# Grouped-query attention on one core: the second tile's K load issued from ScalarE's queue

## Chip, cores and metric

One core of one Trainium2 chip. The metric is device time in microseconds (us) of one launch; lower is better. Before the change the median of 3 runs is 337.94 us (337.85 to 338.18).

## The reference

Attention with 32 query heads that share 8 K/V heads. Only 16 queries per head stand against 2048 keys, so nearly all bytes are K and V (134 MB in bf16).

```python
B, Hq, Hkv, Sq, Sk, D = 16, 32, 8, 16, 2048, 128
k = jnp.repeat(k, Hq // Hkv, axis=1)
v = jnp.repeat(v, Hq // Hkv, axis=1)
scores = jnp.einsum("bhqd,bhkd->bhqk", q, k) * D ** -0.5
p = softmax(scores, axis=-1)
return jnp.einsum("bhqk,bhkd->bhqd", p, v)
```

## The kernel before

The 128 pairs of batch and K/V head are taken two at a time: 64 tiles. A tile needs 1 MB of K and 1 MB of V, and 64 query rows for each of its two heads. The program is written out per engine; semaphores alone order the engines against each other.

For each tile, VectorE transposes K in 32-blocks from `Kd` to `KT` (`kt`, line 421), TensorE forms the scores into `S_ps` (`scores`, line 277), VectorE scales and negates them into `Sneg` and takes the minimum (line 431), ScalarE forms the exponentials into `P` (line 495), TensorE transposes these into `ST_ps` (`turn_p`, line 288), ScalarE copies them to `PT` (line 504), and TensorE multiplies them with V into `O_ps` (`pv`, line 301). ScalarE then divides by the row sums (line 527). Two tiles form a pair: their V loads share one of the two buffers of `Vd`, which come free when the products of the pair before last are formed (`sem_pv`).

Q comes in 16 chunks of 128 KB for four tiles each. GpSimd copies a chunk four times over into `Q4` (line 180), having waited for the load (`sem_q`) and for TensorE's transposes of the chunk before (`sem_qt[1]`); TensorE transposes half a chunk at a time (`turn_q`, line 264) and ScalarE copies the result to `QT` (`q_out`, line 480).

Loads and stores are DMAs, each put into the ring of the engine that issues it. SyncE issues nearly all of them, in the order of a loop over time steps t: K of tile t (`load_k`, line 191; `Kd` has eight slots, so the first eight need no wait, and each later one waits until the transpose of the tile eight before it is done, `sem_kt`), then a chunk of Q (`load_q`, line 217), stores, and V of an earlier tile (`load_v`, line 209; V of tile p goes at t = p + 2 for the first two, p + 6 for the next two, then up to 11 behind). SyncE's first issues are thus K0, K1, K2, Q2, V0, K3, V1, K4 and so on. V of tile 4 is the first V load that has to wait for a buffer. The last six tiles' V go into slots of `Kd`.

ScalarE issues two DMAs only: chunks 0 and 1 of Q, at its very start (line 534), before its table load and its first copies `q_out`. Each load has a semaphore of its own slot that rises by 16 when all has landed (`sem_k[1]` for the K slot of tile 1). VectorE's program begins with `kt(0)` and `kt(1)`, which wait for `sem_k[0]` and `sem_k[1]`, and goes on with the minimum of tile 0, the transpose of tile 2, the minimum of tile 1, and so forth.

Of the kernel before, what the change touches and what calls it, by code (L numbers as in the profile page):

```python
# [6 lines left out]
ALU = mybir.AluOpType  # L7
# [22 lines left out]
def bass_standalone__gqa_softmax__sampling_kernel(  # L30
# [16 lines left out]
    NU = B * Hkv // 2  # L47
# [15 lines left out]
    Kd = sb("Kd", [128, NK, 32 * D], BF16)  # L63
# [21 lines left out]
    sem_k, sem_kt = ring("sem_k", NK), ring("sem_kt", NK)  # L85
# [14 lines left out]
    kf = k.rearrange("b h s d -> (b h s d)").rearrange("(n g i a x) -> n i a g x", n=ND, g=2, i=2, a=64)  # L100
# [4 lines left out]
    def v_lag(p):  # L105
        return 2 if p < 2 else 6 if p < 4 else max(VLAG, 11 - max(p - 6, 0) // 8)
# [11 lines left out]
    for d in range(WHOLE):  # L118
        t = 2 * d + SLAG + v_lag(2 * d + 4)
# [17 lines left out]
    def v_tile(u):  # L137
        return Kd[:, u - T0, :].rearrange("p (g x) -> p g x", g=2)
# [29 lines left out]
    with nc.Block() as block:  # L168
# [16 lines left out]
        @block.sync  # L185
        def _(sp):
            def load_k(m):
                s = m % NK
                if m >= NK:
                    sp.wait_ge(sem_kt[s], m // NK)  # L190
                sp.add_instruction(mybir.InstDMACopy(  # L191
                    name=nc.get_next_instruction_name(), engine=mybir.EngineType.SP,
                    ins=sp.lower_ap_dma(kf[m // 2, m % 2]), outs=sp.lower_ap_dma(Kd[:, s, :].unsqueeze(1)),
                    queue="qSPDynamicHW", mode="Copy", cce_op=ALU.bypass,
                )).then_inc(sem_k[s], 16)

            def load_v(p):
                d, g = divmod(p, 2)
                if p >= T0:
                    sp.wait_ge(sem_kt[p - T0], ROUNDS)  # L200
                    if p < NU - 1:
                        sp.dma_start(v_tile(p), vt[d, g]).then_inc(sem_vt[p - T0], 16)  # L202
                        return
                    for x, (y, lo, hi) in enumerate(LAST_V):
                        sp.dma_start(v_tile(p)[:, y, D * lo:D * hi], vt[d, g, :, y, D * lo:D * hi]).then_inc(sem_vl[x], 16)
                    return
                if d >= NV and g == 0:
                    sp.wait_ge(sem_pv[d % NV], d // NV)
                sp.dma_start(Vd[d % NV][:, g, :, :].rearrange("a j d -> a (j d)"), vf[p]).then_inc(sem_v[d % NV], 16)

            def load_q(c):
                s = c % NQ
                if c >= NQ:
                    sp.wait_ge(sem_q4, c - NQ + 1)
                rows = 128 * QPAIRS
                src = qf[rows * c:rows * (c + 1), :].rearrange("(a j) d -> a j d", j=QPAIRS)
                sp.dma_start(Qn[s][:, :, :], src).then_inc(sem_q[s], 16)

            def store(d, i, g):
                if i == g == 0:  # L220
                    sp.wait_ge(sem_nm[d % NV], normed(d))
                rows = slice(64 * g, 64 * (g + 1))
                sp.dma_start(of[d, i, g], o_sb(d)[rows, i, :]).then_inc(sem_o[d % NO], 16)  # L223

            for t in range(LASTT):
                if t < NU:
                    load_k(t)
                for c in range(2, NQC):
                    if t == max(c, QPAIRS * c - QLEAD):
                        load_q(c)  # L230
                for d, i in store_at.get(t, []):
                    store(d, i, 0)
                for p in v_behind[t]:
                    load_v(p)
                for d, i in store_at.get(t, []):
                    store(d, i, 1)
            for d in range(WHOLE, ND - 1):
                if d < T0 // 2:
                    sp.wait_ge(sem_nm[d % NV], normed(d))
                else:  # L240
                    sp.wait_ge(sem_end, 2 * d + 2 - T0)
                for g in range(2):
                    dst = of[d, :, g].rearrange("i x d -> x i d")
                    sp.dma_start(dst, o_sb(d)[64 * g:64 * (g + 1), :, :]).then_inc(sem_out, 16)
            for i in range(2):
                for g in range(2):
                    sp.wait_ge(sem_end, TILES - 1 + i * (g + 1))
                    sp.dma_start(of[ND - 1, i, g], o_sb(ND - 1)[64 * g:64 * (g + 1), i, :]).then_inc(sem_out, 16)
            for s in range(NO):
                sp.wait_ge(sem_o[s], 64 * ((WHOLE - s + NO - 1) // NO))  # L250
            sp.wait_ge(sem_out, 32 * (ND - WHOLE + 1))
# [224 lines left out]
        @block.scalar  # L476
        def _(act):
            def q_out(x, n):
                act.wait_ge(sem_qt[x], n)
                act.activation(  # L480
                    QT[x][:, :, :].rearrange("p b (a j) -> p b a j", j=QPAIRS),
                    q_ap().rearrange("p b (j a) -> p b a j", j=QPAIRS), ACT.Copy,
                ).then_inc(sem_qe[x], 1)

            def exp(i, alone):
                n = J // 2
                pb, sneg = P[i // 2 % NP][:, :].bitcast(BF16), Sneg[i % 2][:, :]
                for h in range(2 if alone else 1):
                    if alone:
                        dst = pb[:, J * 64 * (i % 2):J * 64 * (i % 2 + 1)].rearrange("p (t y h e) -> p h t y e", t=n // 2, h=2, e=2)[:, h]  # L490
                        src = sneg.rearrange("p (h t e y) -> p h t y e", h=2, t=n // 2, e=2)[:, h]
                    else:
                        dst = pb.rearrange("p (n i y e) -> p i n y e", n=n, i=2, e=2)[:, i % 2]
                        src = sneg.rearrange("p (n e y) -> p n y e", n=n, e=2)
                    ins = act.activation(  # L495
                        dst, src, ACT.Exp, bias=nbias[:, i:i + 1], scale=-1.0,
                        accum_out=rowsum[:, ROUND * h + i:ROUND * h + i + 1],
                    )
                ins.then_inc(sem_exp[i % STEP], 1)

            def p_out(i, n):
                for h in range(2):
                    act.wait_ge(sem_pt[h][i % STEP], n)
                    ins = act.activation(  # L504
                        PT[i % NPT][:, 4 * h:4 * (h + 1), :].rearrange("p t q -> p (t q)"),
                        ST_ps[:, 512 * h:512 * (h + 1)], ACT.Copy,
                    )
                ins.then_inc(sem_po[i % STEP], 1)

            def emit(at):  # L510
                for i in range(ROUND):
                    act.wait_ge(sem_max[i % STEP], at.tile(i))
                    exp(i, at.end and i >= T0 % ROUND)
                    if i % 2 == 0 and not (at.end and i >= 4):
                        y = (i + 4) // 2
                        q_out(y % 2, at.num(2, y // 2 + 1))
                    if at.first or i >= TLAG:
                        p_out(i - TLAG, at.tile(i - TLAG))
                    if i % 2 and (at.first or i >= PVLAG + 1) and not (at.end and i == ROUND - 1):
                        y = (i - PVLAG - 1) // 2  # L520
                        act.wait_ge(sem_pv[y % NV], at.num(2, y // NV + 1))
                        extra = at.end and WHOLE <= ROUND // 2 * (ROUNDS - 1) + y
                        if not extra and (at.first >= 2 or (at.first == 1 and y >= 0)):
                            act.wait_ge(sem_o[y % NO], at.num(64, 64 * (y // NO)))
                        for z in range(2):
                            x = (2 * y + z) % ROUND
                            ins = act.activation(Osb[y % NO + (NO if extra else 0)][:, z, :], o_ap(z), ACT.Copy,  # L527
                                                 scale=rrec[:, x:x + 1])
                        ins.then_inc(sem_nm[y % NV], 1)

            for c in range(2):
                rows = 128 * QPAIRS
                src = qf[rows * c:rows * (c + 1), :].rearrange("(a j) d -> a j d", j=QPAIRS)
                act.dma_start(Qn[c][:, :, :], src).then_inc(sem_q[c], 16)
            for x in range(2):
                q_out(x, 1)
            in_rounds(act, 2, ROUNDS - 1, emit)
            for u in range(NU - TLAG, NU):
                p_out(u, TURNS)
# [28 lines left out]
```

## Time and profile before

| | us or share |
|---|---|
| median of 3 runs | 337.94 |
| profiled execution | 337.78 |
| its span in the profile | 335.9 |
| PE busy (matmul) | 282.2 (84%) |
| VectorE busy | 292.1 (87%) |
| ScalarE busy | 261.8 (78%) |
| GpSimd busy | 31.3 (9%) |
| SyncE's DMA ring (q1): packets, MB | 31632, 138.17 |
| ScalarE's DMA ring (q10): packets, MB | 288, 0.26 |
| DMA over the span | 412 GB/s |
| K load, issue to landing (median) | 11.3 |
| V load, issue to landing (median) | 9.7 |

The span runs from the first to the last instruction that the hardware profiler recorded; the rest of the time lies around it. Busy times are sums over the span, and engines overlap. PE is TensorE's matmul side, PEld its weight load; DVE is VectorE, ACT ScalarE, POOL GpSimd, SP SyncE. Rows with a q behind the engine (SPq, ACTq) are its issues of DMAs, not the movement of the data; the time to landing is from the issue until the data's semaphore is complete, and so contains the wait behind earlier loads of the ring. A DMA share can come out a little over 1 where records overlap. In a row of the timeline the brackets give how long the engine had been idle and what ended that.

### The profile page before, as it was taken

What the parts mean: (1) busy time and instruction counts of PE and PEld (TensorE: products, weight loads), DVE (VectorE), ACT (ScalarE), POOL (GpSimd) and SP (SyncE); (2) the same over time, 40 slices, a digit from 0 to 9 for tenths busy, and PEclk for the clock granted to TensorE, in tenths of its full rate; (3) what the DMA queues carried; (4) which work ended last, traced back from release to release, by engine and by line L of the source; (5) the groups of instructions that cost most, each with busy time, mean ns of one, the idle gap of its engine ahead of it and who ended that gap; (6) DMA issues with size and microseconds to landing.
All of it is one profiled execution on the core that took longest, in us unless ns stands there. A gap on an engine that the chain in (4) does not pass through costs nothing.

```text
span 335.9 us, 14877 instructions
## 1 busy us (share of the span) xinstructions
PE 282.2 (84%) x6720; PEld 164.5 (49%) x6720; DVE 292.1 (87%) x232; ACT 261.8 (78%) x357; POOL 31.3 (9%) x22
## 2 busy tenths in 40 slices
PE   1755888889888889889888898898888889887995
PEld 1323445544554555455445554554455455454484
DVE  2999899998889999999999999999989889889641
ACT  2365888888777889888888888888888877888871
POOL 3202020200202020020202001020201002000000
PEclk9959899999999999999999999999999999999999
DMA  7999999999999999999999999999999999999996
GB/s 300 423 418 417 418 420 416 420 424 424 417 425 423 419 422 422 425 419 413 425 422 421 419 421 424 424 417 420 423 421 424 421 423 424 422 424 424 411 415 212
DMA packets 31930, 138.55 MB, mean 412 GB/s; under 512 B 12464, under 2 KB 14768, under 8 KB 16304
## 3 DMA queue, kind: packets, MB, share of 16 engines
q1 hardware_dynamic: 31632, 138.17, 100.0%
q10 hardware_dynamic: 288, 0.26, 0.2%
q8 instruction: 5, 0.08, 0.1%
q14 instruction: 5, 0.04, 0.0%
HBM read 136.31 MB, written 2.10 MB: 412 GB/s over the span
## 4 chain that ended last, share of the span: by engine, by line
DMA 36%; PE 32%; ACT 15%; SPq 8%; DVE 5%; issue 4%
DMA Vd<-in_v_dram 29%; PE S_ps L277 13%; PE ST_ps L288 9%; PE O_ps L301 9%; ACT P L495 8%; DMA Kd<-in_v_dram 5%; SPq L223 4%; ACT PT L504 3%; DVE Sneg L431 3%; DMA Kd<-in_k_dram 2%; DVE KT L421 2%; ACT QT L480 2%; ACT O L527 2%; SPq L191 2%; SPq L202 1%
## 5 line engine op out<-in xcount | busy, mean ns | idle before, releaser
L495 ACT ACTIVATE P<-Sneg,nbias 128x2048 bf16<-128x2048 f32 (+1 forms) x70 | 161.9, 2315 | 4.1 <-DVE Sneg L431 4.1
L431 DVE TENSOR_SCALAR_CACHE_REDUCE Sneg<-S_ps 128x2048 f32<-128x2048 f32 x64 | 145.3, 2270 | 18.4 <-PE S_ps L277 18.4
L421 DVE STREAM_TRANSPOSE KT<-Kd 128x2048 f32<-128x2048 f32 x64 | 147.4, 2303 | 13.9 <-DMA Kd<-in_k_dram 13.9
L277 PE MATMUL S_ps<-KT,QT 32*64 32x512 bf16 x2048 | 127.7, 623 | 22.3 <-DVE Sneg L431 19.8
L504 ACT ACTIVATE PT<-ST_ps 128x512 f32<-128x512 f32 x128 | 69.6, 595 | 52.2 <-PE ST_ps L288 51.8
L288 PE MATMUL ST_ps<-ident,P 128*128 128x128 f32 x512 | 69.6, 279 | 14.3 <-ACT QT L480 9.6
L301 PEld LDWEIGHTS O_ps<-Vd,PT 64*64 64x64 bf16 x3712 | 54.2, 107 | 37.2 <-issue 36.2
L301 PE MATMUL O_ps<-Vd,PT 64*64 64x128 bf16 x3712 | 63.2, 218 | 8.3 <-DMA Vd<-in_v_dram 8.3
L288 PEld LDWEIGHTS ST_ps<-ident,P 128*128 128x128 f32 x512 | 54.8, 141 | 23.4 <-issue 20.5
L277 PEld LDWEIGHTS S_ps<-KT,QT 32*64 32x64 bf16 x2048 | 29.3, 115 | 73.7 <-issue 45.7
L180 POOL COPY Q<-Qn 128x2048 bf16<-128x2048 bf16 x16 | 30.3, 1896 | 248.9 <-PE ST_ps L264 247.6
L264 PEld LDWEIGHTS ST_ps<-ident,Q 64*128 64x128 f32 x256 | 20.0, 150 | 32.3 <-issue 32.3
L264 PE MATMUL ST_ps<-ident,Q 64*128 64x64 f32 x256 | 24.6, 242 | 5.1 <-POOL Q L180 5.1
L480 ACT ACTIVATE QT<-ST_ps 128x512 f32<-128x512 f32 x32 | 19.5, 610 | 9.3 <-PE ST_ps L264 9.2
L527 ACT ACTIVATE O<-O_ps,rrec 128x128 bf16<-128x128 f32 x56 | 17.7, 376 | 0.0
L495 ACT ACTIVATION_READ_ACCUMULATOR P<-Sneg,nbias 128x1 f32 x70 | 14.4, 206 | 0.0
L431 DVE DVE_READ_ACCUMULATOR Sneg<-S_ps 128x1 f32 x64 | 5.4, 84 | 0.0
L449 DVE TENSOR_SCALAR O<-O_ps,rrec 128x128 bf16<-128x128 f32 (+1 forms) x5 | 1.7, 348 | 3.5 <-PE O_ps L319 2.9
L449 DVE TENSOR_SCALAR O<-S_ps,rrec 128x128 bf16<-128x128 f32 x4 | 1.3, 349 | 3.9 <-PE S_ps L319 3.9
L439 DVE RECIPROCAL rrec<-rowsum 128x2 f32<-128x2 f32 x29 | 4.6, 160 | 0.0
L319 PE MATMUL S_ps<-Kd,PT 128*64 128x128 bf16 x128 | 4.1, 220 | 0.0
L319 PEld LDWEIGHTS S_ps<-Kd,PT 128*64 128x64 bf16 x128 | 3.7, 110 | 0.5 <-issue 0.5
(11 smaller groups left out, 8.2 us busy)
## 6 DMA issues: line engine op xcount, KB each, us to landing
Kd<-in_k_dram SPq DMA_DIRECT2D x64, 1024.0 KB, 11.3
Vd<-in_v_dram SPq DMA_DIRECT2D x58, 1024.0 KB, 9.7
Kd<-in_v_dram SPq DMA_DIRECT2D x5, 1024.0 KB, 13.4
Qn<-in_q_dram SPq DMA_DIRECT2D x14, 128.0 KB, 10.6
out_dram<-O SPq DMA_DIRECT2D x112, 16.0 KB, 9.7
Kd<-in_v_dram SPq DMA_DIRECT2D x1, 512.0 KB, 16.7
Qn<-in_q_dram ACTq DMA_DIRECT2D x2, 128.0 KB, 3.8
Kd<-in_v_dram SPq DMA_DIRECT2D x1, 256.0 KB, 14.1
```

Source lines behind the costliest of these rows:

```text
L180: gp.tensor_copy(Q4[:, :, :, :, :].rearrange("p j b r x -> p (j b) r x"), src.unsqueeze(2).to_broadcast([128, 2 * QPAIRS, 4, 64]),).then_i ...
L223: sp.dma_start(of[d, i, g], o_sb(d)[rows, i, :]).then_inc(sem_o[d % NO], 16)
L264: ins = pe.transpose(q_ap()[:, b, 64 * j:64 * (j + 1)], src[rows, j, b, :], ident[rows, rows])
L277: ins = pe.matmul(S_ps[64 * g:64 * (g + 1), 512 * r:512 * (r + 1)], qt[rows, b, e, at:at + 64], kt[rows, b, e, g], start=(acc == 0), stop= ...
L288: ins = pe.transpose(ST_ps[:, 512 * h + 128 * t:512 * h + 128 * (t + 1)], P[w // 2 % NP][:, 128 * y:128 * (y + 1)], ident[:, :])
L301: ins = pe.matmul(o_ap(i)[64 * g:64 * (g + 1), :], pt[rows, j % 16 // 2, j % 2, 64 * g:64 * (g + 1)], Vd[d % NV][rows, g, j, :], start=(j ...
L421: dve.transpose(KT[u % 2][:, :].rearrange("p (b j a) -> p j b a", b=2, j=J), Kd[:, u % NK, :].bitcast(F32).rearrange("p (j b c) -> p j b c ...
L431: dve.tensor_scalar(Sneg[i % 2][:, :].rearrange("p (j r a) -> p r j a", j=J, r=4), S_ps[:, :].rearrange("p (r j a) -> p r j a", j=J, r=4), ...
L480: act.activation(QT[x][:, :, :].rearrange("p b (a j) -> p b a j", j=QPAIRS), q_ap().rearrange("p b (j a) -> p b a j", j=QPAIRS), ACT.Copy, ...
L495: ins = act.activation(dst, src, ACT.Exp, bias=nbias[:, i:i + 1], scale=-1.0, accum_out=rowsum[:, ROUND * h + i:ROUND * h + i + 1],)
L504: ins = act.activation(PT[i % NPT][:, 4 * h:4 * (h + 1), :].rearrange("p t q -> p (t q)"), ST_ps[:, 512 * h:512 * (h + 1)], ACT.Copy,)
L527: ins = act.activation(Osb[y % NO + (NO if extra else 0)][:, z, :], o_ap(z), ACT.Copy, scale=rrec[:, x:x + 1])
```

## The change

SyncE's loop skips K of tile 1. ScalarE issues that load, with the same source, destination, size and semaphore, into its own ring between its loads of Q chunks 0 and 1. Everything else stays.

```diff
             for t in range(LASTT):
-                if t < NU:
+                if t < NU and t != 1:
                     load_k(t)
...
                 act.dma_start(Qn[c][:, :, :], src).then_inc(sem_q[c], 16)
+                if c == 0:
+                    act.add_instruction(mybir.InstDMACopy(
+                        name=nc.get_next_instruction_name(), engine=mybir.EngineType.Activation,
+                        ins=act.lower_ap_dma(kf[0, 1]), outs=act.lower_ap_dma(Kd[:, 1, :].unsqueeze(1)),
+                        queue="qActDynamicHW", mode="Copy", cce_op=ALU.bypass,
+                    )).then_inc(sem_k[1], 16)
```

## The prediction

> **What bounds the kernel now.** First the page's slices, then stretches of the start beside one of the middle. The first two lines below are the 40 slices (tenths of the 16 DMA engines; GB/s); the others are stretches (length, busy of PE, PEld, DVE, ACT, POOL, granted clock, DMA share, GB/s).
>
> ```profile
> DMA  7999999999999999999999999999999999999996
> GB/s 300 423 418 417 418 420 416 420 424 424 417 425 423 419 422 422 425 419 413 425 422 421 419 421 424 424 417 420 423 421 424 421 423 424 422 424 424 411 415 212
> ...
> 2.00:3.00 1.00, 0.00 (x0) 0.00 (x0) 0.00 (x0) 0.91 (x1) 0.00 (x0) 1.00 1.17 327
> 3.00:4.00 1.00, 0.00 (x0) 0.00 (x0) 0.00 (x0) 0.00 (x0) 0.94 (x1) 1.00 0.82 296
> 4.00:5.00 1.00, 0.00 (x0) 0.00 (x0) 0.00 (x0) 0.00 (x0) 0.96 (x1) 1.00 1.02 420
> 160.00:240.00 80.00, 72.89 (x1819) 42.00 (x1823) 75.16 (x58) 68.18 (x94) 8.09 (x5) 1.00 1.02 422
> ```
>
> The reader is to see one resource that never rests: from the second slice to the last but one the DMA engines are nine tenths busy or more, at some 421 GB/s. A K or V load of 1.05 MB takes 2.49 us at that rate, a tile (one of each) 4.98 us, while VectorE, the busiest compute engine, works 2.31 + 2.27 + 0.08 = 4.66 us a tile. So the end is set by the stream: when it starts, its bytes, whether it ever runs dry, and the tail behind the last V. The change moves none of the bytes and nothing at the tail.
>
> Second, the timeline of the start: issues, then the two K transposes that wait for the loads, then the transpose of tile 4.
>
> ```profile
> 0.72 0.87 ACTq L534 DMA_DIRECT2D Qn<-in_q_dram  x2
> 0.73 1.97 SPq L191 DMA_DIRECT2D Kd<-in_k_dram  x3
> 6.23 2.31 DVE L421 STREAM_TRANSPOSE KT<-Kd 128x2048 f32<-128x2048 f32 x1 [6.23 <-DMA Kd<-in_k_dram]
> 8.98 2.31 DVE L421 STREAM_TRANSPOSE KT<-Kd 128x2048 f32<-128x2048 f32 x1 [0.44 <-DMA Kd<-in_k_dram]
> 11.88 1.90 POOL L180 COPY Q<-Qn 128x2048 bf16<-128x2048 bf16 x1 [6.92 <-PE ST_ps L264]
> 22.94 2.31 DVE L421 STREAM_TRANSPOSE KT<-Kd 128x2048 f32<-128x2048 f32 x1 [0.39 <-DMA Kd<-in_k_dram]
> ```
>
> K0 releases VectorE at 6.23, K1 at 8.98; from there VectorE has no gap until tile 4, whose K it waits 0.39 us for.
>
> Third, SyncE's timeline where loads first wait for computation (V of tiles 4, 6 and 8, each held until the products of an earlier pair of tiles free a buffer of Vd).
>
> ```profile
> 50.71 0.33 SPq L209 DMA_DIRECT2D Vd<-in_v_dram  x1
> ...
> 60.31 0.33 SPq L209 DMA_DIRECT2D Vd<-in_v_dram  x1
> ...
> 69.88 0.33 SPq L209 DMA_DIRECT2D Vd<-in_v_dram  x1
> ```
>
> The list of DMA issues, taken over each of these moments alone, gives issue to landing: 8.3, 8.7 and 9.5 us. K0, issued into empty queues, took 5.5 us. The difference is work still queued ahead when the gate opens: 2.8, 3.2 and 4.0 us. That is how late computation may become before the stream runs dry.
>
> **The change part by part.**
>
> *SyncE loses one issue.* Three K issues take 1.97 us, so one is 0.66, and K2, Q2, V0 and what follows are issued 0.66 us earlier. This is worth nothing: they stand in SyncE's ring behind 1.05 MB of K0, and by 9.73 us SyncE is held by a full ring (the issue of a V there takes 2.13 us instead of 0.48).
>
> *ScalarE gains one issue.* Its two Q issues end at 0.72 + 0.87 = 1.59; with 0.66 more at 2.25. Behind it stands the table load (1.28 us, from 1.62), then to 3.56 at the latest. ScalarE's next work begins at 6.22, when it has waited 3.32 us for TensorE: 2.66 us of cover. Cost 0; without cover 0.66.
>
> *K1 shares the engines with K0 instead of following it.* The trace has no K load in ScalarE's ring, so the price comes from Q1, which stands where K1 will. The DMA queues over 4.2 to 5.4 us (packets, MB, share):
>
> ```profile
> q1 hardware_dynamic: 52, 0.42, 82.5%
> q10 hardware_dynamic: 53, 0.05, 12.7%
> ```
>
> q1 is SyncE's ring with K0 (8 KB packets), q10 ScalarE's with Q1 (1 KB): one packet of each in turn. Q1's first packets come at 3.9 us; before, from 2.6 to 3.9, q10 moved none. By 3.9 us 59 of K0's 128 packets had gone (16 in 1.5 to 2.6, 43 after). If K1 begins at 3.9 too, K0's other 69 packets alternate with 69 of K1: 69 x 8192 B / 421 GB/s = 1.34 us more, less some 0.19 us for Q1's packets that no longer lie between. K0 lands 1.15 us later: the first transpose starts at 7.38 and ends at 9.69. K1's last 59 packets then alternate with K2's: 59 x 8192 / 421 GB/s = 1.15 us more, less Q1's whole 0.35: K1 lands 0.8 us later, its transpose starts at 9.78. VectorE's unbroken row thus begins 0.8 us late.
>
> The bounds: if K1 begins together with K0, K0 comes up to 2.49 - 0.19 = 2.3 us later, the transposes start at 8.53 and 10.84: 1.86 late. If it begins only when K0 is done, it alternates with all of K2: 2.49 - 0.35 = 2.1 late. If its packets keep their old order, 0, and K0 gains the 0.19. So -0.2 to +2.1, and I take 0.8, by the row that is nearest.
>
> The Trainium skill (DMA: Bandwidth & Descriptors, Queues, rings and completion order) says that an engine drains a whole packet of typically 9 to 17 descriptors from one ring before it turns to the other; by that K1's eight pieces on an engine would go in one block, and K0 would be up to 2.5 us late, an estimate that leaves the sum where it is. The one-to-one row above doesn't agree with it.
>
> *Q1 stands behind K1.* It landed at 6.35 (issue 1.15 + 5.2). Now its 8 packets on each engine follow K1 and alternate with K2's and V0's: 8 x 0.35 us (2.49 / 8 for the large one, 0.04 for its own) behind 9.75, so about 12.5. GpSimd reads it at 11.88 + 0.8 = 12.7 at the earliest, since it waits for TensorE; its copy takes 1.90 and TensorE uses the result at 15.60 + 0.8. Cost 0; Q1 would have to land after 14.5 to cost anything.
>
> *Where the lateness goes.* 0.8 us late at tile 1; 0.39 of it falls into the wait at tile 4, as K4's landing hardly moves (the bytes ahead of it are the same). The first gate opens about 0.4 to 0.8 us late, against 2.8 us of queued work: the stream doesn't run dry, V4 and all later loads move at their old times. Behind it the lateness shrinks: gates lie 9.60 and 9.57 us apart, while four loads with their Q and outputs take the stream 9.96 or more, so 0.4 us a pair is made up; the trace shows TensorE waiting for V itself three times between 60 and 100 us (2.5 us in all). K loads that wait for transposes have more cover: the one issued at 39.97 landed 16.6 us later.
>
> *Sum.* Stream start 0, bytes 0, gaps 0, tail 0: against the profiled execution 335.9 us of span plus 1.88 around it = 337.78, which is 0.16 under the median of the runs, 337.94. I forecast no change, 337.9 us. One per cent is 3.4 us; what a measurement here can tell from no change is about 0.2%, 0.68 us.
>
> **Rivals.**
>
> *The stream runs dry at the first gate (slower).* It decides from a delay of 2.8 + 0.39 = 3.2 us at tile 1, and each further us costs one. For: the chain of waits runs through computation from K1's landing to 70 us, PE's granted clock is 0.58 in 15 to 20 and 0.76 in 20 to 40 us, and TensorE once idles 2.10 us there with nothing shown that it waits for; a shifted start could meet such a stall twice. Against: the bound of the landings is 2.1. Price: 2.1 + 2.1 - 3.2 = 1.0 us, 338.9. Were nothing absorbed at all, 0.8 to 2.1 us: 338.7 to 340.0.
>
> *The start fills better (faster).* From 2 to 4 us the engines moved 327 and 296 GB/s against 421: 219 kB missing, 0.52 us. If two rings of large packets fill that, the whole stream moves forward: 337.4. For: the DMA share of 0.82 in 3 to 4 us, when q10 was empty. Against: the share is 1.17 the stretch before, with both rings at work and still 327 GB/s, so the slowness is in the packets. Beyond 0.2% it needs a part of the first 2 us too. The Trainium skill (same page, Issuing engines are not separate DMA queues) speaks against any gain: issuing from two engines saves only the sequencer's time.
>
> *The landings don't move.* K1's descriptors come so late that its packets keep their order: also 337.9, without the delay at the first transposes.
>
> **How the numbers follow.** Forecast 0.59; unmoved landings 0.08; better start 0.14, of which half stays within 0.2%; stream dry 0.19, nearly all of it beyond 0.2%. A little of the forecast's own share is scatter to either side. Faster 0.09, same 0.70, slower 0.21. The range runs from 337.2, a little beyond the full start gain, to 338.9, the dry stream's price.
>
> **What would show it.** Right: first transposes at about 7.4 and 9.8; V4 issued within 1 us of 50.71, its landing sooner behind its issue by the same amount; no slice under nine tenths; last V landing at the old time. Wrong: a dip in GB/s at 50 to 56 us (dry stream), over 327 and 296 GB/s at 2 to 4 us (better start), transposes still at 6.23 and 8.98 (nothing moved), or a Q copy on GpSimd that waits for its load and holds TensorE after 16.4.

## The result, and the profile after

The changed kernel takes 339.77 us (median of 7 runs, 338.92 to 340.40) against 337.85 before (7 runs): ratio 1.0050, 95% interval 1.0035 to 1.0064, so 1.9 us slower. Seven further runs of it gave 339.30 (337.97 to 339.98) against 337.91, ratio 1.0037 (1.0022 to 1.0051). Single runs overlap: the fastest of those seven is about as fast as the kernel before, and among the runs taken beside the experiments 5 of 35 of the kernel before took 339.1 to 339.6, so what follows rests on medians and on the profiles. The forecast of no change was wrong. The profiled execution has a span of 338.4 us, 2.5 more than before.

First the slices of the page after the change (tenths of the DMA engines; GB/s).

```profile
DMA  7999999999999999999999999999999999999996
GB/s 287 421 421 415 418 420 387 367 415 422 422 423 425 412 424 423 423 421 416 423 424 423 422 415 426 423 419 420 421 420 424 422 421 421 422 424 422 413 413 197
```

The tenths are as before, and whoever reads only them sees nothing. The GB/s show two low slices, 387 and 367 (50.8 to 67.7 us), where 416 and 420 stood before. A slice is 8.46 us, so against 421 some 0.75 MB are missing there, 1.8 us of the stream. Everything behind is as fast as before, and none of it is caught up.

The start, from the timeline of the changed kernel:

```profile
0.73 0.40 ACTq L534 DMA_DIRECT2D Qn<-in_q_dram  x1
1.16 0.60 ACTq L536 DMA_DIRECT2D Kd<-in_k_dram  x1
1.80 0.60 ACTq L534 DMA_DIRECT2D Qn<-in_q_dram  x1
8.77 4.72 DVE L421 STREAM_TRANSPOSE KT<-Kd 128x2048 f32<-128x2048 f32 x2 [8.77 <-DMA Kd<-in_k_dram]
13.52 2.29 DVE L431 TENSOR_SCALAR_CACHE_REDUCE Sneg<-S_ps 128x2048 f32<-128x2048 f32 x1
14.32 1.89 POOL L180 COPY Q<-Qn 128x2048 bf16<-128x2048 bf16 x1 [9.47 <-PE ST_ps L264]
24.67 2.29 DVE L421 STREAM_TRANSPOSE KT<-Kd 128x2048 f32<-128x2048 f32 x1
```

The first transpose starts at 8.77 instead of 6.23, the chain of waits puts the second at 11.18 instead of 8.98, and the first minimum (line 431) stands at 13.52 instead of 11.32: VectorE is 2.2 us late. At tile 4 it no longer waits for its K, and is 1.73 late (24.67 against 22.94). The DMA queues over 4.2 to 5.4 us and, below the dots, 6.4 to 8.7 us (packets, MB, share):

```profile
q1 hardware_dynamic: 55, 0.41, 85.5%
q10 hardware_dynamic: 10, 0.08, 19.5%
...
q1 hardware_dynamic: 62, 0.48, 49.8%
q10 hardware_dynamic: 59, 0.48, 49.7%
```

K1, in q10, has moved 10 of its 128 packets by 5.4 us, though it was issued at 1.16. It moves when K0 is all but done, and then one for one with K2, which SyncE has queued behind K0: 59 packets of K1, and of q1 59 of the same size and three small ones.

Below, a gate is the moment at which a V load that had to wait for its buffer is issued, and a hole is a stretch in which the stream of loads moves clearly less than its 421 GB/s. SyncE's first three V loads that wait, and stretches of the stream around them (length, PE, PEld, DVE, ACT, POOL, granted clock, DMA share, GB/s), after the change:

```profile
53.67 0.33 SPq L209 DMA_DIRECT2D Vd<-in_v_dram  x1
63.26 0.33 SPq L209 DMA_DIRECT2D Vd<-in_v_dram  x1
72.83 0.33 SPq L209 DMA_DIRECT2D Vd<-in_v_dram  x1
...
54.00:56.00 2.00, 1.61 (x30) 0.78 (x36) 2.00 (x4) 1.75 (x5) 0.00 (x0) 1.00 0.93 291
...
64.00:68.00 4.00, 3.61 (x100) 1.84 (x101) 4.00 (x5) 4.00 (x7) 0.60 (x1) 1.00 0.95 297
68.00:76.00 8.00, 7.12 (x165) 3.65 (x155) 7.43 (x7) 6.56 (x10) 1.29 (x1) 1.00 1.03 417
```

The same stretches before the change:

```profile
54.00:56.00 2.00, 1.72 (x80) 1.49 (x72) 2.00 (x2) 1.85 (x3) 0.00 (x0) 1.00 1.01 422
...
64.00:68.00 4.00, 3.50 (x101) 2.40 (x107) 4.00 (x3) 2.96 (x6) 1.90 (x1) 1.00 1.02 423
```

Each of the first two gates opens some 2.95 us late and is followed by a hole: 291 GB/s for 2 us (0.62 us of the stream lost against 421) and 297 for 4 us (1.18). Behind the third there is none. Over the first 10 us, 3.08 MB were moved instead of 3.20, 0.27 us more. That is 2.1 of the 2.5 us; 0.4 stays unassigned. In the second profile of this kernel (e5 below) the first 10 us carry 3.20 MB, as before, so the 0.27 us belong to this execution and not to the change as such.

### The profile page after: what moved, and what is told of

It is laid out like the page before. It is cut to its first block, busy times and chain, and to the rows that moved or that the text cites. A ratio compares the mean times of both kernels' runs of the same rounds, so it can differ in the third digit from the quotient of the medians.

```text
span 338.4 us, 14877 instructions
## 1 busy us (share of the span) xinstructions
PE 283.1 (84%) x6720; PEld 165.5 (49%) x6720; DVE 292.0 (86%) x232; ACT 261.8 (77%) x357; POOL 31.3 (9%) x22
## 3 DMA queue, kind: packets, MB, share of 16 engines
q10 hardware_dynamic: 432, 1.31, 1.0%
## 4 chain that ended last, share of the span: by engine, by line
PE 33%; DMA 32%; ACT 17%; SPq 8%; DVE 5%; issue 4%; ACTq 0%
DMA Vd<-in_v_dram 25%; PE S_ps L277 14%; PE ST_ps L288 10%; ACT P L495 10%; PE O_ps L301 9%; DMA Kd<-in_v_dram 4%; ACT PT L504 4%; SPq L223 3%; DMA Kd<-in_k_dram 3%; DVE Sneg L431 3%; ACT QT L480 2%; DVE KT L421 2%; ACT O L527 2%; SPq L202 2%; SPq L191 1%
## 5 line engine op out<-in xcount | busy, mean ns | idle before, releaser
L288 PE MATMUL ST_ps<-ident,P 128*128 128x128 f32 x512 | 70.9, 282 | 15.4 <-ACT QT L480 10.9
L288 PEld LDWEIGHTS ST_ps<-ident,P 128*128 128x128 f32 x512 | 56.1, 143 | 24.4 <-issue 21.4
L319 PE MATMUL O_ps<-Kd,PT 128*64 128x128 bf16 x64 | 3.0, 220 | 1.3 <-DMA Kd<-in_v_dram 1.3
## 6 DMA issues: line engine op xcount, KB each, us to landing
Kd<-in_k_dram SPq DMA_DIRECT2D x63, 1024.0 KB, 11.3
```

What stands on the lines that cost most here:

```text
L288: ins = pe.transpose(ST_ps[:, 512 * h + 128 * t:512 * h + 128 * (t + 1)], P[w // 2 % NP][:, 128 * y:128 * (y + 1)], ident[:, :])
```

## The experiments

Theory of the late start: K1 lands late, VectorE and all behind it start about 2 us late, the first V loads that wait for computation come too late, and the stream runs dry. Rival: it is the move itself that costs, two rings sharing the engines or K's change of ring, and the lateness is absorbed as forecast.

**Lateness without the change (e1_late_one).** The kernel before, all DMAs untouched, with an idle transpose ahead of VectorE's first:

```diff
+    sem_late = sem("sem_late")
...
+            dve.wait_ge(sem_k[0], 16)
+            for x, n in enumerate((32,)):
+                dve.transpose(
+                    KT[0][:, :].rearrange("p (b j a) -> p j b a", b=2, j=J)[:, 0:n],
+                    Kd[:, 0, :].bitcast(F32).rearrange("p (j b c) -> p j b c", b=2, c=32)[:, 0:n],
+                ).then_inc(sem_late, 1)
+                dve.wait_ge(sem_late, x + 1)
             for u in range(2):
                 kt(u, 16)
```

> The kernel before, with VectorE transposing tile 0's K once for nothing ahead of its first transpose (2.31 us); no load is moved, all issues are those of before. Late-start theory: the first transposes that count start at about 8.6 and 10.9 (after the change: 8.8 and 11.1), the V load of tile 4 is issued about 2.7 late, the GB/s dip at 54 to 56 and again at 65 to 68 us, and the time is 1.3 to 2.2 us over before (339.2 to 340.1). Rival (the sharing of the rings itself costs the time, lateness is absorbed): no dip, 337.9 +- 0.3.

Measured: 339.44 against 337.91, ratio 1.0035 (1.0021 to 1.0048). Timeline and stretches of this kernel:

```profile
13.46 2.29 DVE L432 TENSOR_SCALAR_CACHE_REDUCE Sneg<-S_ps 128x2048 f32<-128x2048 f32 x1
53.91 0.33 SPq L210 DMA_DIRECT2D Vd<-in_v_dram  x1
...
54.00:56.00 2.00, 1.61 (x24) 0.95 (x30) 2.00 (x4) 1.59 (x6) 0.00 (x0) 1.00 0.62 201
64.00:68.00 4.00, 3.62 (x85) 1.84 (x87) 4.00 (x5) 3.92 (x6) 0.36 (x1) 1.00 0.95 326
```

The first minimum stands at 13.46, almost where the change put it, the first gate opens at 53.91 (3.2 late, where 2.7 was expected), and both holes are there. A late VectorE alone, with K1 in its old ring, makes the loss.

**Half of it (e2_late_half).** The same with 16 of the 32 blocks.

> The same with half such a transpose (1.16 us): first transposes at about 7.4 and 9.8, the very delay that the prediction reckoned with. Late-start theory with a cover of about 2.8 us at the first gate: gate about 1 us late, no dip, 337.9 +- 0.4. If any lateness costs (no cover): 0.7 to 1.2 us over before. Rival: 337.9.

Measured: 338.21, ratio 1.0003 (0.9986 to 1.0020), not to be told from no change.

```profile
51.81 0.33 SPq L210 DMA_DIRECT2D Vd<-in_v_dram  x1
...
54.00:56.00 2.00, 2.00 (x49) 0.98 (x36) 2.00 (x2) 2.00 (x1) 0.00 (x0) 1.00 1.01 422
64.00:68.00 4.00, 3.51 (x104) 2.44 (x96) 4.00 (x4) 2.96 (x4) 1.89 (x1) 1.00 1.02 423
```

1.1 us late at the gate, and the stream stays whole. There is a cover, that is, a lateness that costs nothing; 1.1 us is within it and 3.2 is not.

**The change with more work queued at the gate (e3_after_k_ahead), and its control (e4_before_k_ahead).** In both kernels V from tile 4 on goes one time step later, behind the K load of that step:

```diff
-        return 2 if p < 2 else 6 if p < 4 else max(VLAG, 11 - max(p - 6, 0) // 8)
+        return 2 if p < 2 else 6 if p < 4 else max(VLAG, 12 - max(p - 6, 0) // 8)
```

> The changed kernel with V loads from tile 4 on one time step later in SyncE's order, so that K of tile 16 is issued ahead of the first V load that waits, and 2.49 us more work is queued when that gate opens. Late-start theory: first transposes still at about 8.8 and 11.1, but no dip at 54 to 56, a smaller one or none at 65 to 68; the time falls to 338.0 to 338.6 (0.2 us of start remain). Rival (sharing itself): stays at 339.8.

> Control of the run before it: the kernel before with the same later V loads. Its stream never ran dry, so late-start theory: 337.9 +- 0.4; where it differs by more, the new order has a price of its own that has to be taken off the run before it.

Measured: 337.86, ratio 0.9987 (0.9973 to 1.0001), and for the control 337.93, 0.9993 (0.9979 to 1.0006). The changed kernel's timeline and stretches in this order:

```profile
13.15 2.29 DVE L431 TENSOR_SCALAR_CACHE_REDUCE Sneg<-S_ps 128x2048 f32<-128x2048 f32 x1
52.45 0.33 SPq L209 DMA_DIRECT2D Vd<-in_v_dram  x1
...
54.00:56.00 2.00, 2.00 (x36) 0.56 (x21) 2.00 (x2) 2.00 (x4) 0.00 (x0) 1.00 1.03 430
64.00:68.00 4.00, 3.13 (x104) 1.69 (x81) 4.00 (x4) 3.18 (x4) 1.82 (x1) 1.00 1.02 419
```

VectorE is 1.8 us late here too, but the holes are gone and with them the whole loss (twelve runs, 337.58 to 338.53); the 0.2 us that were expected to remain don't show. The gate in this profile is 1.7 us late, between e2 and e5, so the claim rests on the twelve times too. The work queued ahead has grown as meant: V of tile 4 lands 9.2 us after its issue, where 8.3 less the 1.7 would be 6.6. The control shows that the order has no price of its own. So the sharing of the rings costs nothing that can be measured, and the rival falls. Nor does the change show a gain where its harm is taken away: neither version can be told from the kernel before.

**The change again (e5_after_again).** The same kernel, profiled once more.

> The changed kernel itself again, to see how much its start differs between executions. Late-start theory: 339.4 to 340.3 with two dips; the second transpose starts at 10.5 to 11.2 us; the landing of K0 may lie anywhere between 6.2 and 8.8, since it hangs on the last of 16 engines, that of K1 hardly moves.

Measured: 339.30, ratio 1.0037 (1.0022 to 1.0051).

```profile
5.96 2.31 DVE L421 STREAM_TRANSPOSE KT<-Kd 128x2048 f32<-128x2048 f32 x1 [5.96 <-DMA Kd<-in_k_dram]
11.11 2.31 DVE L421 STREAM_TRANSPOSE KT<-Kd 128x2048 f32<-128x2048 f32 x1 [2.84 <-DMA Kd<-in_k_dram]
52.83 0.33 SPq L209 DMA_DIRECT2D Vd<-in_v_dram  x1
...
54.00:56.00 2.00, 1.80 (x32) 0.45 (x32) 2.00 (x4) 2.00 (x5) 0.00 (x0) 1.00 1.01 360
64.00:68.00 4.00, 3.51 (x105) 1.88 (x90) 4.00 (x2) 3.57 (x6) 1.44 (x1) 1.00 0.97 291
```

In this execution K0 isn't late at all: 5.96, where the first profile had 8.77. K1 is late as before, at 11.11, VectorE sits idle 2.84 us between the two, and the holes are there. So the two profiles have K1's late landing in common, not K0's. At 2.1 us late the first hole has only begun (360 GB/s).

**Q1 ahead of K1 (e6_k1_last).** The added issue under `if c == 1` instead of `if c == 0`.

> ScalarE issues both Q chunks first and K1 behind them (Q0, Q1, K1). K1's packets begin later, so K0 lands earlier (6.2 to 7.0), but K1 then alternates with K2 and lands 10.8 to 11.3. If VectorE's lateness is set by K1's landing (late-start theory): as late as the change or a little more, two dips, 339.4 to 340.3. If K0's landing is what costs: 337.9 to 338.4.

Measured: 339.82, ratio 1.0064 (1.0052 to 1.0076). K0's transpose stands at 6.38, K1's at 11.72 (10.8 to 11.3 was expected), the gate opens at 53.48, and the stream moves 287 GB/s in 54 to 56 and 342 in 64 to 68 us. K0 is nearly on time and K1 later still, and the loss is there: K1's landing decides.

**Another load in K1's place (e7_k7_instead).** ScalarE issues K of tile 7, `kf[3, 1]`, and SyncE skips that one; K1 is SyncE's second load as before the change.

> ScalarE issues K of tile 7 in that place instead of K1; K1 stays SyncE's second load. The same 1.05 MB shares the engines with K0 and K1, but nothing that VectorE needs soon is in ScalarE's ring. Late-start theory: K0 and K1 land late by what K7 takes off them, the second transpose at about 11, two dips, 339.2 to 340.2. If it is K1's move to the other ring that costs: 337.9 +- 0.3.

Measured: 339.71, ratio 1.0054 (1.0042 to 1.0066).

```profile
5.97 2.31 DVE L421 STREAM_TRANSPOSE KT<-Kd 128x2048 f32<-128x2048 f32 x1 [5.97 <-DMA Kd<-in_k_dram]
11.21 2.31 DVE L421 STREAM_TRANSPOSE KT<-Kd 128x2048 f32<-128x2048 f32 x1 [2.93 <-DMA Kd<-in_k_dram]
```

K1's transpose is as late as when K1 itself was moved; K0, which was expected late, isn't. It doesn't matter which of two loads stands in which ring: behind K0 two loads of 1.05 MB share the engines, and the second tile's ends with both (K7 lands 9.9 us after its issue at 1.16).

**Twice the lateness (e8_late_two).** As e1, with two idle transposes.

> The kernel before with two idle transposes (4.6 us) ahead of VectorE's first. Late-start theory: past the point where the stream runs dry each further us costs about one: e1's 1.5 over before and 2.3 more, 341.7 (341.0 to 342.4). If the loss is a fixed price of two restarts: 339.4 as e1.

Measured: 341.07 (4 runs, 339.91 to 342.40), ratio 1.0106 (1.0088 to 1.0125): 1.63 us over e1 for 2.3 us more at the start. The loss grows with the lateness and is no fixed price; with four runs spread over 2.5 us, how steeply isn't known. The profiled execution is the fastest of the four: its first minimum stands at 15.48, 2.0 behind that of e1, but its gate at 54.64, only 0.7 behind.

**Stores away from the second gate (e9_after_stores_later), and the control (e10_before_stores_later).** `SLAG = 8` instead of 6 in both kernels.

> The changed kernel with all stores of the main loop two time steps later, so that none stands beside the V load of tile 6. It asks what makes the second dip (65 to 68 us), larger than the first though the gate there had more work queued. If the stores between the gate and that V load's data make it: the second dip shrinks from 1.2 us to under 0.5, the first stays at 0.3 to 0.7, and the time falls to 338.3 to 339.0. If it is lateness alone: both dips stay, 339.3 to 339.9.

> Control of the run before it: the kernel before with the same later stores. No dip in either case; 337.9 +- 0.4, and what it differs by is the price of the new order.

Measured: 339.33, ratio 1.0041 (1.0027 to 1.0055); control 337.79, 0.9998 (0.9988 to 1.0007). The changed kernel moves 225 GB/s in 54 to 56 us and 334 in 64 to 68. The second hole stays (0.83 us of the stream, where under 0.5 was expected if the stores made it), so the stores aren't its main cause.

## Why the prediction was wrong

Gate, holes and time of the profiled executions side by side; "late" is against 50.71, lost stream is (421 - GB/s) x length / 421, the last column the median of all runs less that of before.

| kernel | first minimum | gate, late | lost in 54-56 | lost in 64-68 | time over before |
|---|---|---|---|---|---|
| before | 11.32 | 50.71, 0 | 0 | 0 | 0 |
| e2, half transpose | 12.41 | 51.81, 1.1 | 0 | 0 | 0.30 (not told from 0) |
| e3, one more K queued ahead | 13.15 | 52.45, 1.7 | 0 | 0 | -0.05 |
| change, e5 | 13.46 | 52.83, 2.1 | 0.29 | 1.24 | 1.39 |
| e7, K7 instead | 13.55 | 53.49, 2.8 | 0.66 | 0.92 | 1.80 |
| e6, K1 last | 14.07 | 53.48, 2.8 | 0.64 | 0.75 | 1.91 |
| change | 13.52 | 53.67, 3.0 | 0.62 | 1.18 | 1.92 |
| e9, stores later | 13.28 | 53.80, 3.1 | 0.93 | 0.83 | 1.46 |
| e1, one transpose | 13.46 | 53.91, 3.2 | 1.05 | 0.90 | 1.53 |
| e8, two transposes | 15.48 | 54.64, 3.9 | 1.28, and 0.38 in 56-58 | 0.44 | 3.16 |

The last column doesn't rise evenly, because the other columns are of one execution and this one is of all. The profiled executions' own times do fit their holes: against the 337.78 of before they are longer by 1.5 (e5), 2.1 (e7), 2.0 (e6), 2.5 (the change), 2.1 (e9), 2.3 (e1) and 2.1 us (e8), which is what the holes in a row add up to, or up to 0.7 more.

Two steps failed, and either alone would have left the forecast at no change.

*K1's landing: the term was mis-sized.* The prediction let K1's packets begin at 3.9 us, where Q1's had begun, took K0 1.15 and K1 0.8 us later, and VectorE 0.8. K1 began only when K0 was nearly through and shared with the whole of K2: the case named as a bound, 2.1 late. Measured 1.8 to 2.2 in the four profiles with this start (second transpose at 10.81 in e3, 10.94 in e9, 11.11 in e5, 11.18 after the change; 8.98 before). Q1 was a poor stand-in for when a larger load in that ring begins. K0 was late in one of these four profiles (8.77; the others 5.96 to 6.33); the loss doesn't hang on it.

*The cover at the first gate: the step that failed.* "That is how late computation may become before the stream runs dry" was 2.8 us, 3.2 with the wait at tile 4. The runs put it between 1.1 (whole) and 2.1 us (first hole). The 5.5 us of K0 was taken as the landing of a load in empty queues, and the difference as queued work. But V of tile 4 still landed 6.2 us after its issue in e5, with the hole already open.

The trace's records of semaphores (no view prints them) show why. A load's semaphore rises in sixteen steps, read here as the sixteen DMA engines finishing their shares. Before the change, the K load issued last ahead of the gate (at 39.97) has twelve steps at 54.57 to 55.20 and four at 56.24 to 56.53; V of tile 4 has twelve at 57.06 to 57.71 and four at 58.73 to 59.01. After the change the twelve of V come at 57.99 to 58.54, 0.8 to 0.9 us late, and the four at 58.81 to 59.20, at most 0.2 late. So twelve shares run dry while the four that set the landing hardly move: a landing tells only of the last. Taken from the first step instead (V 6.35 us after its issue, K0 4.89), the prediction's own subtraction gives 1.5 us of cover, between the 1.1 and 2.1 of the runs. And the time from the gate to the first step of the K load queued ahead orders the holes: 3.9 us before and 2.7 in e2 (no hole), 1.7 in e5 (0.29), 1.1 after the change (0.62), 0.6 in e1 (1.05).

*The second gate was given 3.2 us of cover, and it failed too.* Nothing in the prediction had a hole there once the first had pushed the stream back. That V load landed 7.1 us after its issue and still left 1.18 us of hole. Why it takes longer than at the first gate isn't settled; only the stores were tried.

*Between start and gate: nothing was absorbed.* The prediction let 0.39 us fall into VectorE's wait at tile 4. That wait went, but it was not on the path: the chain of waits goes by TensorE, which begins the scores of that moment at 24.73 instead of 22.53, still 2.2 us late. VectorE's next minimums that wait for TensorE, before and, below the dots, after:

```profile
30.07 2.29 DVE L431 TENSOR_SCALAR_CACHE_REDUCE Sneg<-S_ps 128x2048 f32<-128x2048 f32 x1 [0.41 <-PE S_ps L277]
35.42 2.29 DVE L431 TENSOR_SCALAR_CACHE_REDUCE Sneg<-S_ps 128x2048 f32<-128x2048 f32 x1 [0.77 <-PE S_ps L277]
...
32.18 2.29 DVE L431 TENSOR_SCALAR_CACHE_REDUCE Sneg<-S_ps 128x2048 f32<-128x2048 f32 x1 [0.80 <-PE S_ps L277]
38.35 2.29 DVE L431 TENSOR_SCALAR_CACHE_REDUCE Sneg<-S_ps 128x2048 f32<-128x2048 f32 x1 [1.58 <-PE S_ps L277]
```

1.73 late at tile 4 is 2.11 at the first of them, so the 0.39 us are back, and 2.93 at the second; the gate is 2.96 late. In e2, e5 and e6 what stood at the first minimum (1.1, 2.1, 2.75) stands unchanged at the gate. The 0.8 us more at the second minimum lie in TensorE's eight transposes ahead of it (line 288): they took 1.97 us at a granted clock of 0.51, against 1.31 at 0.78 before, and began after an idle stretch 0.16 longer (2.26 against 2.10). In e5 they took 1.09 at 1.00. The stretches of lower clock lie differently in each execution (0.83 in 30 to 40 us in both these profiles, 0.88 in e5), and of the nine late profiles only four grew so between start and gate (the change, e1, e7, e9). It looks like scatter between executions; that the change has no hand in it isn't shown. The rival that named such a stall had the place and the mechanism right (the stream dry at the first gate), but decided from 3.2 us and was given 0.19.

*Right:* no cost from SyncE's and ScalarE's issues (the table load moved from 1.62 to 2.43, ScalarE's first copy stands at 6.12), none from Q1 (GpSimd's copy at 14.32 was released by TensorE); the gates stay 9.59 and 9.57 us apart, less than the 9.96 us that the stream takes for as much, so they gain on it and no third hole follows; a fuller start did not come. "No slice under nine tenths" came true as well, and was no sign that the stream was whole. With the cover sized right, the lateness of 2.1 us that was named as a bound would have meant a loss.

## What to carry to other kernels

In this kernel, bound by its loads, a delay of computation was free only while every DMA engine still had work queued when computation freed the next buffer. In another such kernel, find the first load that waits for computation and size that cover by a small idle delay, not by landing times, which tell of the last engine. Two transfers side by side didn't come sooner together: the second ended when both ended, so the load that is needed next belonged behind the first in one ring, with nothing beside it. Where such a gate is tight, an order that puts a load that needs no wait ahead of the waiting one buys the cover back (e3: all of the 1.9 us).

## What the runs showed of the hardware

- K1's first packets came over 3 us after ScalarE's issue (issued at 1.16; 10 packets between 4.2 and 5.4 us, none in 2.6 to 4.2), while the Q chunk issued 0.43 us ahead of it landed 2.2 us after its issue.
- 8 KB packets of the two rings get equal turns: 59 of each in 6.4 to 8.7 us after the change. In e6 and e7 the records of single packets show sixteen of one ring, then sixteen of the other, again and again.
- The shares of one load don't end together: before the change the sixteen steps of the semaphore of V of tile 4 spread over 1.95 us (57.06 to 59.01).
- Around a hole the DMA share can stay high (0.93 at 291 GB/s, 0.95 at 297, after the change) or fall (0.62 at 201, e1). A hole shows in GB/s; in the tenths of the 40 slices after the change it doesn't show at all. In the records of single packets some of the first 8 KB packets behind the gates last 0.7 to 1.4 us at the first and up to 1.9 us at the second, instead of 0.31, and all of that time counts as busy. What such a packet waits for, the records don't say.
